# Later query loads and the adapter on the GpSimd queue, stores split into four pieces

## The chip, the cores and the metric

The kernel runs on one core of a Trainium2 chip. The metric is device time in microseconds of one launch, from inputs in device memory to outputs in device memory. The core has five engines that run side by side, each with its own instruction stream in order: TensorE (PE in the profile, with its weight loads as PEld), VectorE (DVE), ScalarE (ACT), GpSimd (POOL) and SyncE (SP), which here only issues transfers. Transfers are issued on the queues of SP, ACT and POOL and carried out by 16 DMA engines. Results of TensorE land in PSUM; everything else lies in SBUF.

## The reference

Two stages, in float32. The first is a retention layer on q, k, v of shape (8 batches, 8 heads, 576 positions, 64): scores are scaled by 1/8, multiplied by a decay gamma_h^(i-j) for i >= j and zero otherwise, and applied to v without a softmax. Its output, seen as x of 4608 tokens by 512 columns, goes into a mixture of adapters: 8 experts of rank 16.

```
scores = scale * q @ k.T                      # per batch and head
ret    = scores * Dmat                        # gamma_h ** (i - j), i >= j, else 0
x      = (ret @ v) as (4608, 512)
logits = x @ w_gate                           # 8 experts
top 2 experts per token, softmax weights w over these two
out    = x + sum over the two: w * ((x @ A[e]) @ B[e])
```

## The kernel before, in words

The positions are cut into chunks of 128, four full ones and a rest of 64. A *unit* is one chunk of two batches (for the rest chunk, of four batches), with all 8 heads; there are 18 units, numbered 0 to 17, in two runs of nine. The decay is split into factors of rows and columns, so that the unit's keys are scaled once (`k_scale`, L226, in place in the loaded tile) and the output once (`xT_out`, with the tables gx). What earlier chunks add is kept as a running state W per batch and head.

For a unit u the work is:

- loads of q, k and v into natural tiles of 256 KB per batch, two transfers per tensor and unit (`load`, `load_batch`, L139 to L169). The tiles have 3, 4 and 4 buffers; `freed(u, name)` (L171) is the point at which the tile of unit u is free, and issues the load of unit u + 3 (queries) or u + 4 (keys, values) into its buffer. All of these are on SP's queue, except two of unit 0's on ACT's.
- `k_scale` on GpSimd, then transposes of keys and queries on TensorE (`T_mm`, L248), copied out by ScalarE (`k_out`, `q_out`, `qs_out`) into kT, M and Qs. `q_turn` (L271) copies half of Qs into M; it is on GpSimd (L185, M<-Qs).
- scores (`S0_mm` L322, `S1_mm` L304), masked by VectorE into M and S1 (L373, L360).
- `W_values` and `V1_copy` put v beside the state on GpSimd (L185, W<-v and V<-v); `U_mm` (L395) makes k^T v, which `U_out` adds to the state of the chunk behind it: one half on VectorE, the other by a ScalarE copy and a GpSimd add (L188, W<-pn,W).
- outputs x^T (`O_mm` L432, `O1_mm` L451), scaled by VectorE; router and adapter product in one (`Z_mm`, L487) against AW, which holds A and w_gate; the routing on VectorE and ScalarE; B applied and x added back (`Y_mm` L605, `B_mm` L620); osb copied out and stored (`store`, L691).

The order on every engine is written out by hand: the order of the calls in the program is the order of each engine's stream, and waits follow from data. Units 0 to 3 are written out one by one (L803 to L948); from r = 2 on, a loop (L954) works on unit r's outputs, unit r + 1's scores and unit r + 2's transposes. The last two units' outputs stand behind the loop.

The adapter A is loaded once into An and put into the layout of AW by TensorE (`A_select`, L514) with a selection table sel, which `A_select_open` (L496) builds on GpSimd from ident: a memset and 16 small copies (L503). Bcat and Wg are the two loads on GpSimd's queue. W has zero halves for the first chunks, written by four memsets (L207) for units 0 and 1.

The lines ahead of the first scores of unit 0, where the changed loads are issued:

```
    load(1, "k")
    load(1, "q")
    nc.sync.dma_start(
        out=An.rearrange("p e i r -> p e (i r)"),
        in_=moe_A.rearrange("e (a i) r -> a e (i r)", i=4),
    )
    load(1, "v")
    ...
    for nm, u in (("k", 2), ("q", 2), ("v", 2), ("k", 3), ("q", 3), ("v", 3)):
        load(u, nm)
```

Of the kernel before, what the change touches and what calls it, by code (L numbers as in the profile page):

```python
# [17 lines left out]
HALF = (LO, HI)  # L18
# [3 lines left out]
def kernel(  # L22
# [10 lines left out]
    nc = tc.nc  # L33
    B, H, S, Dh = q.shape
    Ntok, Dm = out.shape
    E = moe_w_gate.shape[1]
    R = moe_A.shape[2]
    ER = E * R
# [57 lines left out]
    ident = cpool.tile([128, 128], FP32, tag="ident", name="ident")  # L96
# [12 lines left out]
    AW = rest.tile([128, HP, ER + E], FP32, tag="AW", name="AW")  # L109
    Bcat = cpool.tile([128, Dm], FP16, tag="Bcat", name="Bcat")  # L110
    ident16 = rest.tile([128, 128], FP16, tag="ident16", name="ident16")
    warm = rest.tile([128, 1], FP32, tag="warm", name="warm")
    An = cpool.tile([128, E, 4, R], FP32, tag="An", name="An")
    Wg = rest.tile([128, HP, E], FP32, tag="Wg", name="Wg")
# [8 lines left out]
    NU = len(units)  # L123
# [15 lines left out]
    def load_batch(u, nm, b, eng=None):  # L139

        c, bp = units[u]
        return (eng or nc.sync).dma_start(  # L142
            out=nat[(nm, u)][:, b * H : (b + 1) * H, :],
            in_=srcs[nm][2 * bp + b, :, 128 * c : 128 * c + 128, :].rearrange("h j d -> j h d"),
        )

    def load_open(u, nm):
        nat[(nm, u)] = iop.tile(
            [128, 2 * H, Dh], FP32, tag=nm + "32", name=nm + "32", bufs=NBUF[nm]
        )  # L150

    def load(u, nm):

        if u >= NU:
            return
        load_open(u, nm)
        c, bp = units[u]
        if full(u):
            for b in range(2):
                load_batch(u, nm, b)  # L160
            return
        for par in range(2):
            b = 4 * bp + 2 * par
            nc.sync.dma_start(
                out=nat[(nm, u)][HALF[par]],
                in_=srcs[nm][b : b + 2, :, 128 * c : 128 * c + 64, :].rearrange(
                    "b h j d -> j (b h) d"
                ),
            )  # L169

    def freed(u, nm):  # L171

        load(u + NBUF[nm], nm)
# [25 lines left out]
    def W_open(u):  # L199
        n = 1 if full(u) else 2  # L200
        st[u]["W"] = [
            wk.tile([128, 2, 2, HP, Dh], FP32, tag=f"W{x}", name=f"W{x}", bufs=(5, 2)[x])
            for x in range(n)
        ]
        if units[u][0] == 0:
            for p in range(2):
                nc.gpsimd.memset(st[u]["W"][0][HALF[p], p], 0.0)  # L207

    def W_values(eng, u, ps=(0, 1)):
        vt = nat[("v", u)]  # L210
# [5 lines left out]
    def V1_copy(eng, u):  # L216

        s = st[u]
        s["V1"] = wk.tile([64, 2, HP, Dh], FP32, tag="V1", name="V1", bufs=2)
        for b, src in enumerate(heads(nat[("v", u)][HI], 0)):  # L220
            copy(eng, s["V1"][:, b], src)

    def k_scale(eng, u, bs=slice(0, 2)):
        c = units[u][0]
        kt = nat[("k", u)].rearrange("p (b h) d -> p b h d", b=2)[:, bs]
        eng.tensor_tensor(  # L226
            out=kt, in0=kt,
            in1=gv[:, c, :].unsqueeze(1).unsqueeze(3).broadcast_to(
                (128, bs.stop - bs.start, H, Dh)
            ),  # L230
            op=ALU.mult,
        )
# [38 lines left out]
    def q_turn(eng, u, p):  # L271

        s = st[u]
        copy(
            eng, s["M"][HALF[p], p, 1],
            s["Qs"][HALF[1 - p]].rearrange("p a r i -> p a (r i)"),
        )
# [202 lines left out]
    def Z_open(u, tag="F"):  # L480
        st[u]["pz"] = bank(tag, [128, 2, ER + E], name="pz")
# [14 lines left out]
    def A_select_open(eng):  # L496


        eng.memset(sel, 0.0)
        for g in range(2):  # L500
            for e in range(2):
                for i in range(4):
                    eng.tensor_copy(  # L503
                        out=sel[HALF[g], e, i, :].rearrange("p (a x) -> p a x", x=4)[:, :, i],
                        in_=ident[HALF[g], 64 * g + 32 * e : 64 * g + 32 * e + 32],
                    )

    def A_select(tags, engs):

        pa = [bank(t, [128, 2, E, R], name="pa") for t in tags]  # L510
        for e in range(2):
            for i in range(4):
                for g in range(2):
                    mm(  # L514
                        pa[g][:, e].rearrange("p a r -> p (a r)"),
                        lhsT=sel[HALF[g], e, i, :],
                        rhs=An[HALF[g], :, i, :],
                        start=(e == 0 and i == 0),
                        stop=(i == 3),
                        skip_group_check=True,  # L520
                    )
        for g in range(2):
            copy(
                engs[g], AW[:, 2 * g : 2 * g + 2, 0:ER],
                pa[g].rearrange("p e a r -> p e (a r)"),
            )
# [164 lines left out]
    def store(u):  # L691
        c, bp = units[u]
        of = st[u]["osb"]
        tok = out.rearrange("(b s) d -> s b d", s=S)
        if full(u):
            for n in range(2):
                nc.sync.dma_start(
                    out=tok[128 * c : 128 * c + 128, 2 * bp + n, :], in_=of[:, n, :]
                )
            return  # L700
        for par in range(2):
            b = 4 * bp + 2 * par
            nc.sync.dma_start(
                out=tok[128 * c : 128 * c + 64, b : b + 2, :], in_=of[HALF[par]]
            )
# [98 lines left out]
    for b in range(2):  # L804
        d = load_batch(0, "v", b)
        if b == 0:
# [4 lines left out]
                ),  # L811
                reason="first keys and queries",
            )
    load(1, "k")
    load(1, "q")
    nc.sync.dma_start(
        out=An.rearrange("p e i r -> p e (i r)"),
        in_=moe_A.rearrange("e (a i) r -> a e (i r)", i=4),
    )
    load(1, "v")  # L820
    T_first("q", 0, "S")
    for p in range(2):
        copy(
# [6 lines left out]
    T_first("q", 1, "EF")  # L830
    for r in range(2):
        copy(nc.scalar, s0["Qs"][:, :, r], pt[("q", 1)][r])
    for nm, u in (("k", 2), ("q", 2), ("v", 2), ("k", 3), ("q", 3), ("v", 3)):
        load(u, nm)
    T_first("k", 1, "R")
    k_first(1)
# [10 lines left out]
    W_values(nc.gpsimd, 0, (0,))  # L847
    W_values(nc.scalar, 0, (1,))
    V1_copy(nc.gpsimd, 0)
    A_select_open(nc.gpsimd)  # L850
    k_scale(nc.vector, 1)
    U_mm(0)
    freed(0, "k")
# [8 lines left out]
    k_out(nc.scalar, 1)  # L862
    T_open(1, "q", "R")
    T_mm(1, "q")
    freed(1, "q")
    q_out(nc.vector, 1, 0)
    for b in range(2):
        xT_out(0, slice(b, b + 1))
# [1 line left out]
    qs_out(nc.scalar, 1)  # L870
    for p in range(2):
        q_turn(nc.gpsimd, 1, p)
    A_select("EF", (nc.scalar, nc.scalar))
    nc.gpsimd.tensor_copy(out=AW[:, :, ER : ER + E], in_=Wg)
    nc.gpsimd.tensor_copy(out=ident16, in_=ident)
    S0_mm(1, "S")
    S1_mm(1, "R")
    for b in range(2):
# [2 lines left out]
    S1_mask(1)  # L881
    W_values(nc.gpsimd, 1)
    V1_copy(nc.gpsimd, 1)
    Z_open(0)
    Z_mm(0)
    U_mm(1)
# [18 lines left out]
    k_out(nc.scalar, 2)  # L905
    T_open(2, "q", "S")
    T_mm(2, "q")
    freed(2, "q")
    q_out(nc.scalar, 2, 0)
    q_out(nc.scalar, 2, 1)  # L910
    qs_out(nc.scalar, 2)
    for p in range(2):
        q_turn(nc.gpsimd, 2, p)
    Z_open(1, "E")
    Z_mm(1)
    route_a(1)
# [19 lines left out]
    k_out(nc.scalar, 3)  # L936
    T_open(3, "q", "R")
    T_mm(3, "q")
    freed(3, "q")
    q_out(nc.scalar, 3, 0)  # L940
    q_out(nc.scalar, 3, 1)
    qs_out(nc.scalar, 3)
# [2 lines left out]
    V1_copy(nc.gpsimd, 3)  # L945
    for p in range(2):
        q_turn(nc.gpsimd, 3, p)
    k_scale(nc.gpsimd, 4)  # L948


# [3 lines left out]
    for r in range(2, END):  # L954
        nxt, nn = r + 1, r + 2
        if full(nxt):
            U_mm(nxt, "E" if r > 2 else "F")
        freed(nxt, "k")
        if full(nxt):
            U_out(nxt)  # L960
        O_mm(r)
        O1_mm(r)
        freed(r, "v")
        if full(nxt):
            xT_out(r)
        else:
            for b in range(2):
                xT_out(r, slice(b, b + 1))
        if full(nxt):
            S1_mm(nxt, "R")  # L970
            S1_mask(nxt)
        S0_mm(nxt)
        for p in range(2):
            S0_mask(nxt, p)
        X_mm(r - 1)
        zT_out(r - 1)
        Z_open(r)
        Z_mm(r)
        route_a(r)
        early = nn < NU and not full(nn)  # L980
        if not early:
            Y_mm(r - 1, "R")
        if nn < NU:
            if "W" not in st[nn]:
                W_open(nn)
            T_open(nn, "k", "A")
            T_mm(nn, "k")
            k_out(nc.scalar, nn)
        if early:
            Y_mm(r - 1, "R")  # L990
        route_s(r)
        B_mm(r - 1)
        osb_open(r - 1)
        osb_out(nc.vector if nn < NU else nc.scalar, r - 1)
        store(r - 1)
        if nn < NU:
            T_open(nn, "q", "S")
            T_mm(nn, "q")
            freed(nn, "q")
            q_out(nc.scalar, nn, 0)  # L1000
            q_out(nc.scalar, nn, 1)
            qs_out(nc.scalar, nn)
            W_values(nc.gpsimd, nn)
            if full(nn):
                V1_copy(nc.gpsimd, nn)
            for p in range(2):
                q_turn(nc.gpsimd, nn, p)
            if nn + 1 < NU:
                k_scale(nc.gpsimd, nn + 1)
            if r < 2 * NFULL and r % 2 == 0:  # L1010
                gx_of(r // 2 + 1)
        route_b(r)
# [81 lines left out]
```

## Time and profile before

| what | value |
|---|---|
| median of 3 runs | 185.77 us |
| all runs | 183.97, 185.77 and 916.15 us |
| the profiled execution's own time | 183.94 us |
| its span | 182.2 us |
| instructions | 9356 |
| moved by DMA | 39.00 MB, mean 214 GB/s |
| read and written in device memory | 29.09 MB and 9.44 MB |

The span runs from the first to the last instruction of one profiled execution; the 1.74 us around it belong to the execution's own time. Busy shares are of the span. In the lines by slices, each digit is the busy share of one fortieth of the span, 4.6 us, in tenths; PEclk is the granted clock of TensorE. A timeline row is: start, duration, engine, line, operation, output<-input with shapes, how many are merged, and in brackets how long the engine sat idle before it and what ended that. `x2` rows are two instructions merged.

### The profile page before, as it was taken

The numbers are of one execution on the slowest core, as the hardware profiler recorded it, in microseconds if no ns is written. First come the engines' busy times: TensorE is split into PE (matmuls) and PEld (weight loads), VectorE is DVE, ScalarE is ACT, GpSimd is POOL, SyncE is SP. The second block draws the span as 40 slices with busy tenths as digits, with TensorE's granted clock in tenths as the row PEclk, the third lists the DMA queues.
The fourth block names the chain that finished last, engine by engine and source line by source line (L and its number), as shares of the span: only waits on it lengthen the run. The fifth ranks groups of instructions, "written<-read, shape, count | busy, mean of one in ns | idle before, by whom it ended". The sixth has DMA issues, their size and how long they took to land.

```text
span 182.2 us, 9356 instructions
## 1 busy us (share of the span) xinstructions
PE 173.1 (95%) x4126; PEld 157.8 (87%) x4126; DVE 128.8 (71%) x232; ACT 76.3 (42%) x156; POOL 125.1 (69%) x214
## 2 busy tenths in 40 slices
PE   7998999599999999999999999999999999999980
PEld 6797998498999899998999999999999999989960
DVE  4494763718686869696868596969696969687770
ACT  0734164910707070706273634343444444443330
POOL 7396984998297959796987747858677777792000
PEclk9999999969999999999999999999999999999997
DMA  4999899899997979999989798989999999923125
GB/s 115 288 229 211 182 199 206 181 235 227 219 286 175 255 176 267 219 288 230 270 185 271 173 293 193 258 183 246 220 286 232 264 202 271 273 84 119 55 107 189
DMA packets 119368, 39.00 MB, mean 214 GB/s; under 512 B 114320, under 2 KB 114720, under 8 KB 119328
## 3 DMA queue, kind: packets, MB, share of 16 engines
q1 hardware_dynamic: 116480, 37.30, 82.9%
q10 hardware_dynamic: 2672, 0.96, 2.1%
q8 instruction: 32, 0.52, 1.1%
q0 software_dynamic: 176, 0.15, 0.5%
q14 instruction: 8, 0.07, 0.1%
HBM read 29.09 MB, written 9.44 MB: 212 GB/s over the span
## 4 chain that ended last, share of the span: by engine, by line
PE 87%; POOL 4%; DMA 3%; SPq 2%; DVE 0%; issue 0%; DVEq 0%
PE pz L487 18%; PE px L432 17%; PE pu L395 9%; PE ps L322 8%; PE pt_k L248 5%; PE px L451 5%; PE po L620 5%; PE pt_q L248 4%; PE po L605 4%; PE ps L304 4%; PE pf L723 3%; DMA v<-in_v_dram 3%; SPq L142 2%; PE pzt L587 2%; POOL sel L503 2%; PE pa L514 1%
## 5 line engine op out<-in xcount | busy, mean ns | idle before, releaser
L373 DVE TENSOR_TENSOR M<-ps,tri 64x1024 f32<-64x1024 f32 (+1 forms) x34 | 37.3, 1097 | 3.8 <-PE ps L322 3.1
L487 PE MATMUL pz<-AW,xT 128*128 128x136 f32 x288 | 37.7, 284 | 0.0
L226 POOL TENSOR_TENSOR k<-k,pack 128x1024 f32<-128x1024 f32 (+1 forms) x18 | 32.5, 1806 | 6.6 <-PE pt_k L779 2.9
L185 POOL COPY M<-Qs 64x512 f32<-64x512 f32 x36 | 21.9, 609 | 21.9 <-ACT Qs L183 16.1
L432 PE MATMUL px<-M,W 128*64 128x128 f32 (+1 forms) x640 | 36.1, 268 | 0.0
L185 POOL COPY W<-v 64x256 f32<-64x256 f32 x78 | 29.2, 395 | 10.0 <-DMA v<-in_v_dram 6.8
L487 PEld LDWEIGHTS pz<-AW,xT 128*128 128x128 f32 x288 | 34.6, 190 | 0.4
L183 ACT COPY kT<-pt_k 128x1024 f32<-128x1024 f32 x17 | 17.2, 1015 | 40.1 <-PE pt_k L248 40.1
L432 PEld LDWEIGHTS px<-M,W 128*64 128x64 f32 x640 | 32.8, 141 | 0.2
L470 DVE TENSOR_TENSOR xT<-px,gx 128x1024 f32<-128x1024 f32 x11 | 13.5, 1225 | 17.8 <-PE px L451 13.4
L185 DVE COPY osb<-po 128x1024 f32<-128x1024 f32 (+2 forms) x18 | 19.2, 1075 | 5.9 <-PE po L620 5.0
L596 ACT COPY zT<-pzt 128x256 f16<-128x256 f16 (+1 forms) x19 | 6.9, 361 | 37.7 <-PE pzt L587 37.7
L183 ACT COPY M<-pt_q 64x512 f32<-64x512 f32 x35 | 20.2, 577 | 1.8 <-DVE M L185 0.7
L395 PE MATMUL pu<-v,k 128*64 128x64 f32 x512 | 19.2, 229 | 1.6 <-DMA v<-in_v_dram 1.6
L395 PEld LDWEIGHTS pu<-v,k 128*64 128x64 f32 x512 | 16.8, 141 | 3.0 <-ACT kT L183 1.4
L322 PE MATMUL ps<-Qs,kT 64*64 64x128 f32 (+1 forms) x304 | 17.9, 259 | 0.0
L322 PE MATMUL ps<-M,kT 64*64 64x128 f32 (+1 forms) x304 | 17.9, 259 | 0.0
L188 POOL TENSOR_TENSOR W<-pn,W 64x512 f32<-64x512 f32 x12 | 15.2, 1270 | 0.9
L322 PEld LDWEIGHTS ps<-M,kT 64*64 64x64 f32 x304 | 14.8, 134 | 0.2
L322 PEld LDWEIGHTS ps<-Qs,kT 64*64 64x64 f32 x304 | 14.8, 134 | 0.0
L248 PEld LDWEIGHTS pt_k<-ident,k 64*128 64x128 f32 x272 | 9.8, 138 | 3.7 <-issue 2.5
L248 PE MATMUL pt_k<-ident,k 64*128 64x64 f32 x272 | 12.1, 229 | 0.5 <-POOL k L226 0.5
(73 smaller groups left out, 295.7 us busy)
## 6 DMA issues: line engine op xcount, KB each, us to landing
q<-in_q_dram SPq DMA_DIRECT2D x36, 256.0 KB, 5.2
v<-in_v_dram SPq DMA_DIRECT2D x36, 256.0 KB, 4.7
k<-in_k_dram SPq DMA_DIRECT2D x34, 256.0 KB, 4.7
out_dram<-osb SPq DMA_DIRECT2D x34, 256.0 KB, 4.6
k<-in_k_dram ACTq DMA_DIRECT2D x2, 256.0 KB, 4.9
An<-in_moe_A_dram SPq DMA_DIRECT2D x1, 256.0 KB, 5.4
out_dram<-osb ACTq DMA_DIRECT2D x2, 128.0 KB, 2.8
out_dram<-osb SPq DMA_DIRECT2D x2, 128.0 KB, 2.9
```

Source lines behind the costliest of these rows:

```text
L183: nc.scalar.copy(out=out, in_=in_)
L185: eng.tensor_copy(out=out, in_=in_)
L188: eng.tensor_tensor(out=out, in0=a, in1=b, op=ALU.add)
L226: eng.tensor_tensor(out=kt, in0=kt, in1=gv[:, c, :].unsqueeze(1).unsqueeze(3).broadcast_to((128, bs.stop - bs.start, H, Dh)), op=ALU.mult,)
L248: mm(ps[:, r, hp, b, :], lhsT=src[HALF[r], b * H + 2 * hp : b * H + 2 * hp + 2, :], rhs=ident[HALF[r], 64 * r : 64 * r + 64], is_transpose ...
L322: mm(s["ps0"][HALF[1 - p], b, hp, sl], lhsT=s["kT"][HALF[ho], x, hp, b, :], rhs=Q_of(u, b, ho, hp, sl), start=(hp == 0 and x == 0), stop=True,
L373: nc.vector.tensor_tensor(out=s["M"][sl, p, bs].rearrange("p b a i -> p (b a) i"), in0=s["ps0"][sl, bs].rearrange("p b a i -> p (b a) i"), ...
L395: mm(s["pu"][HALF[p], b, hp, :], lhsT=nat[("k", u)][:, h, :], rhs=nat[("v", u)][:, h, :], start=(hp == 0 and b == 0), stop=True, skip_grou ...
L432: mm(s["pxb"][b][HALF[ho], hp, sl], lhsT=s["W"][x][:, p, b, hp, :], rhs=s["M"][:, p, b, hp, sl], start=(hp == 0 and x == 0), stop=True, sk ...
L451: mm(s["px"][HALF[ho], b, hp, HI], lhsT=vv, rhs=s["S1"][HALF[p], b, hp, :], start=False, stop=True, skip_group_check=True,)
L470: nc.vector.tensor_tensor(out=s["xT"][:, bs].rearrange("p b a i -> p b (a i)"), in0=s["px"][:, bs].rearrange("p b a i -> p b (a i)"), in1= ...
L487: mm(s["pz"][:, n, :], lhsT=s["xT"][:, n, dt, :], rhs=AW[:, dt, :], start=(dt == 0), stop=(dt == HP - 1), skip_group_check=True,)
```

## The change

- Queries of units 2 and later are loaded by GpSimd's queue, not SP's. Each load stands at another place of the order: unit 2's behind unit 1's `q_turn`, unit 3's behind unit 1's `V1_copy`, unit 4's behind unit 2's `q_turn`, those of 5 and 6 behind unit 3's `q_turn` and ahead of `k_scale` of unit 4; in the loop the load stands behind `q_turn` (that is, behind `V1_copy` on GpSimd) and ahead of the next `k_scale`.
- The adapter A is loaded by GpSimd's queue, behind `V1_copy` of unit 0.
- `A_select_open`, the copy of Wg into AW and ident16 stand at the head of GpSimd's stream; the memsets of W of units 0 and 1 are on VectorE.
- In the loop, `q_turn` is on ScalarE.
- A full unit's two stores (128 rows each) become four, of 104 and 24, and of 88 and 40 rows, except for the last two units.

```
@@ load
+        eng = nc.gpsimd if nm == "q" and u > 1 else nc.sync
...
-                load_batch(u, nm, b)
+                load_batch(u, nm, b, eng)
...
-            nc.sync.dma_start(
+            eng.dma_start(
@@ W_open
-                nc.gpsimd.memset(st[u]["W"][0][HALF[p], p], 0.0)
+                (nc.vector if u < 2 else nc.gpsimd).memset(st[u]["W"][0][HALF[p], p], 0.0)
@@ store
-            for n in range(2):
-                nc.sync.dma_start(
-                    out=tok[128 * c : 128 * c + 128, 2 * bp + n, :], in_=of[:, n, :]
-                )
+            for n, cut in enumerate((104, 88)):
+                for a, b in ((0, cut), (cut, 128)) if u < NU - 2 else ((0, 128),):
+                    nc.sync.dma_start(
+                        out=tok[128 * c + a : 128 * c + b, 2 * bp + n, :], in_=of[a:b, n, :]
+                    )
@@ start
-    load(1, "k")
-    load(1, "q")
-    nc.sync.dma_start(
-        out=An.rearrange("p e i r -> p e (i r)"),
-        in_=moe_A.rearrange("e (a i) r -> a e (i r)", i=4),
-    )
-    load(1, "v")
+    for nm in "kqv":
+        load(1, nm)
+    A_select_open(nc.gpsimd)
+    nc.gpsimd.tensor_copy(out=AW[:, :, ER : ER + E], in_=Wg)
+    nc.gpsimd.tensor_copy(out=ident16, in_=ident)
...
-    for nm, u in (("k", 2), ("q", 2), ("v", 2), ("k", 3), ("q", 3), ("v", 3)):
+    for nm, u in (("k", 2), ("v", 2), ("k", 3), ("v", 3)):
...
     V1_copy(nc.gpsimd, 0)
-    A_select_open(nc.gpsimd)
+    nc.gpsimd.dma_start(
+        out=An.rearrange("p e i r -> p e (i r)"),
+        in_=moe_A.rearrange("e (a i) r -> a e (i r)", i=4),
+    )
...
     T_mm(1, "q")
-    freed(1, "q")
...
         q_turn(nc.gpsimd, 1, p)
+    load(2, "q")
     A_select("EF", (nc.scalar, nc.scalar))
-    nc.gpsimd.tensor_copy(out=AW[:, :, ER : ER + E], in_=Wg)
-    nc.gpsimd.tensor_copy(out=ident16, in_=ident)
...
     V1_copy(nc.gpsimd, 1)
+    load(3, "q")
...
     T_mm(2, "q")
-    freed(2, "q")
...
         q_turn(nc.gpsimd, 2, p)
+    freed(1, "q")
...
     T_mm(3, "q")
-    freed(3, "q")
...
         q_turn(nc.gpsimd, 3, p)
+    freed(2, "q")
+    freed(3, "q")
     k_scale(nc.gpsimd, 4)
@@ loop
             T_mm(nn, "q")
-            freed(nn, "q")
...
             for p in range(2):
-                q_turn(nc.gpsimd, nn, p)
+                q_turn(nc.scalar, nn, p)
+            freed(nn, "q")
             if nn + 1 < NU:
                 k_scale(nc.gpsimd, nn + 1)
```

## The prediction

> **What bounds the kernel now.** I read the page first: engine shares, then the slices, then the chain that ended last.
>
> ```profile
> PE 173.1 (95%) x4126; PEld 157.8 (87%) x4126; DVE 128.8 (71%) x232; ACT 76.3 (42%) x156; POOL 125.1 (69%) x214
> PE   7998999599999999999999999999999999999980
> PEclk9999999969999999999999999999999999999997
> DMA  4999899899997979999989798989999999923125
> PE 87%; POOL 4%; DMA 3%; SPq 2%; DVE 0%; issue 0%; DVEq 0%
> ```
>
> TensorE is the bound, apart from slice 7 (half busy), slice 8 (lower clock) and the last two. The table of stretches puts times on this.
>
> ```profile
> 30.00:33.00 3.00, 2.54 (x76) 1.93 (x66) 1.29 (x3) 1.53 (x5) 1.90 (x1) 1.00 0.82 188
> 33.00:36.24 3.24, 1.55 (x37) 1.31 (x37) 3.06 (x7) 2.85 (x5) 2.87 (x4) 1.00 0.76 168
> 36.24:41.30 5.06, 5.06 (x108) 4.89 (x112) 0.68 (x1) 0.88 (x2) 4.85 (x8) 0.66 1.03 233
> 47.00:56.04 9.04, 9.04 (x232) 8.38 (x234) 7.09 (x13) 3.90 (x10) 6.60 (x9) 1.00 0.93 230
> 99.90:145.10 45.20, 45.20 (x1152) 41.89 (x1152) 34.82 (x60) 19.99 (x42) 32.06 (x50) 1.00 0.96 237
> ```
>
> Columns: span, busy time of PE, PE's weight loads, DVE, ACT, POOL, granted clock, DMA share, GB/s. From 47 us on TensorE is full: one unit takes 9.04 us, and five of them 45.20. Nothing in the diff touches those matmuls, so the change can gain only ahead of 47 us. There TensorE idles 0.46 + 1.69 us and then runs 5.06 us at clock 0.66, which loses (1 - 0.66) x 5.06 = 1.7 us. The TensorE timeline says what it waited for:
>
> ```profile
> 16.14 2.06 PE L514 MATMUL pa<-An,sel 64*128 64x128 f32 x32 [0.34 <-POOL sel L503]
> ...
> 25.13 0.72 PE L248 MATMUL pt_k<-ident,k 64*128 64x64 f32 x16
> ...
> 33.05 0.71 PE L248 MATMUL pt_k<-ident,k 64*128 64x64 f32 x16 [0.50 <-POOL k L226]
> ...
> 35.55 0.34 PE L395 MATMUL pu<-v,k 128*64 128x64 f32 x4 [1.29 <-DMA v<-in_v_dram]
> 36.24 1.01 PE L395 MATMUL pu<-v,k 128*64 128x64 f32 x18 [0.35 <-DMA v<-in_v_dram]
> ...
> 45.27 0.71 PE L248 MATMUL pt_k<-ident,k 64*128 64x64 f32 x16
> ```
>
> The three L248 rows are the key transposes of units 2, 3 and 4. Each needs its unit's keys scaled by Pool (L226). Without waits, unit 2 to unit 3 takes 33.05 - 0.50 - 25.13 = 7.42 us. Unit 3 to unit 4 takes 12.22, less 1.64 of waits and 1.7 of clock, so 8.88. I use the start of unit 4's key transpose, 45.27 us now, as the finish line: all behind it is 9.04 us a unit.
>
> **The change, part by part.** *Off SP's queue.* The sync queue now issues adapter and queries ahead of unit 3's values:
>
> ```profile
> 10.60 2.64 SPq L816 DMA_DIRECT2D An<-in_moe_A_dram  x1
> ...
> 25.81 3.72 SPq L142 DMA_DIRECT2D q<-in_q_dram  x2
> 29.57 1.79 SPq L142 DMA_DIRECT2D v<-in_v_dram  x2
> ```
>
> Without 2.64 and 3.72 us the values are issued over 6 us sooner, so the 1.64 us wait goes. The bytes stay, so some of this returns as sharing with the Pool queue; 1.64 of cover in 6 is enough. The rule against this part: the Trainium skill, "DMA: Bandwidth & Descriptors", section "Issuing engines are not separate DMA queues", says a second issuer gives no bandwidth, only issue time. By it the values come sooner only by order, and the sum stays; the trace, with a DMA share of 0.93 from 47 us, agrees as far as it goes.
>
> *The price on Pool.* A DMA issued by Pool is work on Pool. The trace has two:
>
> ```profile
> 1.27 0.95 POOL L732 DMA_DIRECT2D Wg<-in_moe_w_gate_dram  x1 [0.82 <-POOLq L1078]
> ...
> 23.87 0.59 POOL L890 DMA_DIRECT2D Bcat<-in_moe_B_dram  x1
> ...
> Bcat<-in_moe_B_dram POOLq DMA_DIRECT2D x1, 128.0 KB, 4.3
> ...
> Wg<-in_moe_w_gate_dram POOLq DMA_DIRECT2D x1, 16.0 KB, 4.7
> ```
>
> Bcat has 128 pieces, one row each; Wg has 512 pieces of 32 B. A query load has 1024 pieces of 256 B. If only the instruction counts, c, the cost of one, is 0.59 to 0.95. If pieces count, the two rows give 0.36 us per 384, and c = 0.95 + 512 x 0.36 / 384 = 1.43; twice Wg gives 1.9. Bounds 0.59 and 1.9. I take the middle of the two rows, 0.77: in size the load is nearer to Bcat, in pieces to Wg. This is the choice on which the time hangs.
>
> The skill's "SBUF — State Buffer", section "SBUF: two separate sides", has another price: such an issue took about 620 ns alone and 3100 behind a VectorE copy within SBUF; the page would make c 3.1 there. No run here shows it. VectorE's copies after the start read PSUM.
>
> Now Pool's order from the first q_turn of unit 1, by starts of the rows:
>
> ```profile
> 17.80 1.26 POOL L185 COPY M<-Qs 64x512 f32<-64x512 f32 x2 [1.40 <-ACT Qs L183]
> ...
> 19.63 1.51 POOL L185 COPY W<-v 64x256 f32<-64x256 f32 x4
> 21.20 0.74 POOL L185 COPY V<-v 64x256 f32<-64x256 f32 x2
> 22.03 1.90 POOL L226 TENSOR_TENSOR k<-k,pack 128x1024 f32<-128x1024 f32 x1
> ...
> 24.48 1.05 POOL L746 TENSOR_TENSOR gx<-gkx,pack 128x512 f32<-128x512 f32 x1
> ...
> 33.05 1.26 POOL L185 COPY M<-Qs 64x512 f32<-64x512 f32 x2
> 34.39 1.26 POOL L188 TENSOR_TENSOR W<-pn,W 64x512 f32<-64x512 f32 x1
> ...
> 39.49 1.90 POOL L226 TENSOR_TENSOR k<-k,pack 128x1024 f32<-128x1024 f32 x1
> ```
>
> After the change, start at 17.9 (the queries of unit 1 are no sooner). Then q_turn(1) 1.3; q(2) 2c; W(1) 1.6, V1(1) 0.8; q(3) 2c; k_scale(2) 1.9: done at 23.5 + 4c. Bcat 0.6, gx 1.1, W(2) 1.6, V1(2) 0.8, k_scale(3) 2.0: 29.6 + 4c. q_turn(2) 1.3, q(4) 2c, the add (L188) 1.3, W(3) 1.6, V1(3) 0.7, q_turn(3) 1.3, q(5) and q(6) 4c, k_scale(4) 1.9: **37.7 + 10c**. Ten query issues stand ahead of unit 4's keys, where the row at 39.49 ends at 41.4 today, 3.9 us before use.
>
> With c = 0.77 the scaled keys of unit 2 are there at 26.6 (25.13 today), of unit 3 at 32.7, of unit 4 at 45.4. TensorE: transposes of unit 2 at 26.6, of unit 3 at 34.0, ready for unit 4 at 42.9, and waits until 45.4, against 45.27: +0.1. This idle stretch, 2.5 us, is longer than the 1.69 after which the clock fell today, so I add its 1.7 us again. Behind it: per unit Pool has 6.60 - 1.25 + 1.54 = 6.9 us of 9.04 and doesn't hold TensorE again. The query issue waits there for the transposes of the queries; behind it stand the key scaling and the next add, which used to wait for the longer chain through ACT's Qs copy.
>
> *q_turn on ACT from unit 4 on.* Two copies a unit:
>
> ```profile
> 111.05 0.58 ACT L183 COPY pn<-pu 64x512 f32<-64x512 f32 x1
> 114.04 0.37 ACT L596 COPY zT<-pzt 128x256 f16<-128x256 f16 x1 [2.42 <-PE pzt L587]
> ```
>
> The pn copy comes 1.2 us later, inside the 2.42 us of idle: nothing. Without that cover 1.2 us a unit, 17 in all.
>
> *Start.* The memsets of W, 2.2 us on Pool, go to VectorE; the selection table, AW and ident16 come forward, so the 0.34 us at 16.14 goes. But the adapter now leaves Pool only behind V1(0), at about 12.2 to 13.0, and with 4.3 to 4.7 us to land it is there at 16.5 to 17.7: TensorE loses 0.4 to 1.6 us at 16.14. At c = 0.77 the key scaling of unit 2, 1.5 us late, covers it; at less than 0.6 it is what remains. VectorE and Pool also get in each other's way:
>
> ```profile
> 22.91 1.03 DVE L547 SCALAR_TENSOR_TENSOR ns<-m 128x2 f32<-128x2 f32 x1
> ...
> 28.72 0.16 DVE L547 SCALAR_TENSOR_TENSOR ns<-m 128x2 f32<-128x2 f32 x1
> ```
>
> The slow one ends with Pool's scaling at 23.93. VectorE's start tables would now meet Pool's selection copies in this way, 0 to 1.5 us; it delays the adapter more than TensorE, and is in its bound.
>
> *Stores in four.* Two more issues a unit on SP, which lost two query issues; bytes the same. I cost it at nothing; the rival below prices it.
>
> The sum: profiled execution 183.94 us (span 182.2 and 1.74 around it) + 0.1 + 1.7 = **185.7**. This sits on the profiled execution; the median shown, 185.77 (183.97 to 916.15), is 1% above it, and about 2% is what a measurement of this kernel can tell from no change.
>
> **The rivals.** *Cheap issues* (c up to 0.6). Unit 4's keys are scaled by 43.7, at most. TensorE could be there at 25.13 + 0.4 to 1.6 + 7.42 + 8.88 = 41.8 to 43.0, without idle stretch or clock loss. That is 1.6 to 3.5 us sooner, 180.5 to 182.3. For it: Bcat's 0.59 for the same order of bytes. Against: Wg's 0.95 for fewer.
>
> *Pieces count* (c about 1.43; it decides from c = 0.95). The keys of unit 4 come at 37.7 + 14.3 = 52.0: +6.7, with the clock 190.6 to 192.3, slower. In the loop Pool would then need 8.2 us of 9.04, still inside. At c = 0.95 it is 47.2 and 1.7 of clock, 187.5. For it: the only two rows rise with the pieces. Against: the Wg row is the first of its kind on Pool.
>
> *Stores on fewer DMA engines.* Rows of 104, 24, 88 and 40 may not spread evenly.
>
> ```profile
> 16.20:21.70 5.50, 5.50 (x114) 5.18 (x114) 3.85 (x7) 1.81 (x4) 3.83 (x12) 1.00 0.87 197
> ...
> 176.00:180.00 4.00, 1.11 (x13) 0.55 (x12) 1.61 (x4) 0.86 (x3) 0.00 (x0) 0.99 0.69 240
> ```
>
> Loads alone run at 197 / 0.87 = 226 GB/s full, stores alone at 348. A unit's 1.57 MB in and 0.52 MB out are 6.9 + 1.5 = 8.4 us of 9.04. If the stores lie on 13, 12, 11 and 10 engines, the fullest ten carry 8 + 2 + 8 + 4 = 22 rows for 16: 6.9 + 2.1 = 9.0, just at the limit. Were Pool's query loads a tenth slower in the engines as well, 0.2 us a unit over 14 units adds 3: 188.7. The Trainium skill, "DMA: Bandwidth & Descriptors", "Why a DMA increments its semaphore by 16 and not by 1", says the engines are the largest number up to 16 that divides the rows, which is these four counts; no trace here shows it.
>
> **How the numbers follow.** Forecast (c from 0.6 to 0.95, 183.9 to 187.5): 0.45. Cheap issues: 0.22. Pieces count: 0.25. Stores at the limit: 0.08. Range 180.8 to 191.5. Faster by over 2% (under 180.3) is the best end of the cheap case: 0.13. Slower by over 2% (over 187.6): pieces, stores and the forecast's edge: 0.37. Within: 0.50.
>
> **What would show it.** Right: Pool's query rows at 0.6 to 0.95 us; no wait for v at unit 3; TensorE waiting for k L226 at units 2 and 4; one stretch of lower clock behind; 9.04 us a unit after 47. Wrong: Pool rows of 1.4 us, a wait for An over 1.6 us, stretches over 9.1 us in the middle with waits for DMA, or slack at unit 4's keys.

## The result: slower, and where the time went

The changed kernel takes 191.48 us (189.86 to 193.93, 4 runs) beside 186.48 us of the kernel before on the same chip, a ratio of 1.043 (95% interval 1.032 to 1.054). Run again on another chip, it took 189.79 beside 185.41: 1.026 (1.016 to 1.036). The profiled execution has a span of 188.1 us; before it was 182.2, so 5.9 us are to be found. Medians here take in all runs; the ratios leave out disturbed executions, so the two can differ.

The page of the changed kernel: shares, slices, chain.

```profile
PE 175.0 (93%) x4126; PEld 159.4 (85%) x4126; DVE 134.2 (71%) x236; ACT 94.1 (50%) x184; POOL 134.9 (72%) x215
...
PE   7998969995999999999998999899999999999990
...
PEclk9999996999699999999999999999999999999997
...
PE 75%; POOL 9%; DVE 4%; ACT 4%; issue 3%; DMA 2%; SPq 0%; DVEq 0%; POOLq 0%
```

Before, one slice was at the lower clock; now there are two, with a slice ahead of each in which TensorE is less than full. Pool's share of the chain has gone from 4% to 9%, and "issue", time without a cause in the profile, is at 3%. TensorE's timeline names the waits.

```profile
16.13 2.06 PE L515 MATMUL pa<-An,sel 64*128 64x128 f32 x32 [0.33 <-DMA An<-in_moe_A_dram]
...
26.83 0.71 PE L249 MATMUL pt_k<-ident,k 64*128 64x64 f32 x16 [1.64 <-POOL k L227]
...
47.25 0.71 PE L249 MATMUL pt_k<-ident,k 64*128 64x64 f32 x16 [2.53 <-POOL k L227]
...
99.54 0.27 PE L305 MATMUL ps<-M,kT 64*64 64x64 f32 x1 [0.98 <-issue]
```

The wait for unit 3's values isn't there. In its place TensorE waits for scaled keys, at unit 2 and, longer, at unit 4. Line numbers are one higher than before. Why the keys are late is in Pool's timeline, start and duration first:

```profile
19.02 1.76 POOL L142 DMA_DIRECT2D q<-in_q_dram  x2
20.77 1.53 POOL L186 COPY W<-v 64x256 f32<-64x256 f32 x4
22.36 0.75 POOL L186 COPY V<-v 64x256 f32<-64x256 f32 x2
23.05 1.76 POOL L142 DMA_DIRECT2D q<-in_q_dram  x2
24.88 1.90 POOL L227 TENSOR_TENSOR k<-k,pack 128x1024 f32<-128x1024 f32 x1
...
34.03 1.84 POOL L142 DMA_DIRECT2D q<-in_q_dram  x2
...
41.70 3.53 POOL L142 DMA_DIRECT2D q<-in_q_dram  x4
45.30 1.90 POOL L227 TENSOR_TENSOR k<-k,pack 128x1024 f32<-128x1024 f32 x1
```

Each scaling of keys (L227) ends just ahead of the transposes above: 26.78 and 47.20. Right ahead of both stand query issues. What an issue costs is in Pool's groups:

```profile
L142 POOL DMA_DIRECT2D q<-in_q_dram x28 | 25.2, 902 | 12.8 <-PE pt_q L249 12.6 <-issue 0.2
...
L851 POOL DMA_DIRECT2D An<-in_moe_A_dram x1 | 0.9, 947 | 0.0
L735 POOL DMA_DIRECT2D Wg<-in_moe_w_gate_dram x1 | 0.9, 932 | 0.8 <-POOLq L1082 0.8
L893 POOL DMA_DIRECT2D Bcat<-in_moe_B_dram x1 | 0.6, 602 | 0.0
```

The table of stretches (span, busy time of PE, weight loads, DVE, ACT, POOL, granted clock, DMA share, GB/s) sorts the rest. The rows at clock 0.50 and 0.51 follow the two waits for keys.

```profile
28.40:31.80 3.40, 3.40 (x19) 3.15 (x19) 0.12 (x2) 1.84 (x4) 3.17 (x8) 0.50 0.89 181
44.70:47.25 2.55, 0.03 (x1) 0.00 (x0) 2.48 (x4) 0.00 (x0) 2.43 (x2) 1.00 0.91 257
48.80:52.20 3.40, 3.40 (x54) 3.33 (x52) 2.31 (x5) 3.31 (x8) 3.32 (x8) 0.51 1.16 304
57.85:93.04 35.19, 35.19 (x890) 32.36 (x890) 27.51 (x48) 20.14 (x39) 30.26 (x44) 1.00 0.94 233
93.04:103.25 10.21, 9.23 (x232) 8.43 (x232) 7.18 (x13) 5.76 (x11) 9.26 (x18) 1.00 0.99 253
112.30:122.09 9.79, 9.31 (x232) 8.45 (x232) 7.80 (x16) 5.15 (x10) 7.20 (x10) 1.00 0.93 235
```

The same two units in the kernel before, in the same table:

```profile
89.49:98.16 8.67, 8.67 (x231) 8.11 (x230) 6.49 (x12) 4.38 (x9) 7.91 (x15) 1.00 0.89 224
116.25:125.30 9.05, 9.05 (x231) 8.38 (x231) 7.09 (x13) 3.91 (x8) 6.65 (x10) 1.00 0.93 217
```

So of the 5.9 us, 2.0 are there when unit 4's keys are transposed (47.25 against 45.27). 1.6 come in the unit behind it, at the lower clock, which takes 10.6 us up to 57.85 for 9.04. And 1.5 + 0.7 come in the two units of 10.21 and 9.79 us, most of it in gaps that no wait explains. The remaining 0.1 is in smaller pieces.

### The profile page after: what moved, and what is told of

Read it like the earlier page. It is cut to its first block, busy times and chain, and to the rows that moved or that the text cites. A ratio compares the mean times of both kernels' runs of the same rounds, so it can differ in the third digit from the quotient of the medians.

```text
span 188.1 us, 9337 instructions
## 1 busy us (share of the span) xinstructions
PE 175.0 (93%) x4126; PEld 159.4 (85%) x4126; DVE 134.2 (71%) x236; ACT 94.1 (50%) x184; POOL 134.9 (72%) x215
## 3 DMA queue, kind: packets, MB, share of 16 engines
q1 hardware_dynamic: 82370, 28.65, 62.5%
q0 software_dynamic: 2816, 8.80, 16.5%
## 4 chain that ended last, share of the span: by engine, by line
PE 75%; POOL 9%; DVE 4%; ACT 4%; issue 3%; DMA 2%; SPq 0%; DVEq 0%; POOLq 0%
PE pz L488 16%; PE px L433 15%; PE pu L396 8%; PE ps L323 6%; PE pt_k L249 5%; PE po L621 5%; PE px L452 4%; PE pt_q L249 4%; PE po L606 4%; PE ps L305 3%; POOL q L142 3%; DMA q<-in_q_dram 2%; POOL k L227 2%; PE pzt L588 2%; POOL W L186 1%
## 5 line engine op out<-in xcount | busy, mean ns | idle before, releaser
L488 PE MATMUL pz<-AW,xT 128*128 128x136 f32 x288 | 39.5, 292 | 0.5 <-issue 0.5
L488 PEld LDWEIGHTS pz<-AW,xT 128*128 128x128 f32 x288 | 36.1, 196 | 1.1 <-issue 0.7
L142 POOL DMA_DIRECT2D q<-in_q_dram x28 | 25.2, 902 | 12.8 <-PE pt_q L249 12.6
L227 POOL TENSOR_TENSOR k<-k,pack 128x1024 f32<-128x1024 f32 (+1 forms) x18 | 32.5, 1804 | 1.3 <-PE pt_k L782 0.2
L396 PEld LDWEIGHTS pu<-v,k 128*64 128x64 f32 x512 | 17.1, 144 | 1.3 <-issue 0.3
L184 ACT COPY M<-Qs 64x512 f32<-64x512 f32 x28 | 17.3, 617 | 0.6
L249 PEld LDWEIGHTS pt_k<-ident,k 64*128 64x128 f32 x272 | 9.9, 138 | 8.0 <-POOL k L227 4.6
L249 PE MATMUL pt_k<-ident,k 64*128 64x64 f32 x272 | 12.1, 229 | 4.7 <-POOL k L227 4.2
```

The lines of the kernel that those rows point to most:

```text
L142: return (eng or nc.sync).dma_start(out=nat[(nm, u)][:, b * H : (b + 1) * H, :], in_=srcs[nm][2 * bp + b, :, 128 * c : 128 * c + 128, :].r ...
L184: nc.scalar.copy(out=out, in_=in_)
L227: eng.tensor_tensor(out=kt, in0=kt, in1=gv[:, c, :].unsqueeze(1).unsqueeze(3).broadcast_to((128, bs.stop - bs.start, H, Dh)), op=ALU.mult,)
L249: mm(ps[:, r, hp, b, :], lhsT=src[HALF[r], b * H + 2 * hp : b * H + 2 * hp + 2, :], rhs=ident[HALF[r], 64 * r : 64 * r + 64], is_transpose ...
L396: mm(s["pu"][HALF[p], b, hp, :], lhsT=nat[("k", u)][:, h, :], rhs=nat[("v", u)][:, h, :], start=(hp == 0 and b == 0), stop=True, skip_grou ...
L488: mm(s["pz"][:, n, :], lhsT=s["xT"][:, n, dt, :], rhs=AW[:, dt, :], start=(dt == 0), stop=(dt == HP - 1), skip_group_check=True,)
```

## The experiments

Three theories stood at the start. **A**: Pool's query issues delay the keys, and the clock falls behind each wait. **B**: the four stores load some DMA engines more. **C**: Pool's large transfers delay the fetching of instructions in the middle. A ratio is always to the kernel before on the same chip.

**Keys first.** The changed kernel with three of the early loads moved:

```
-    load(3, "q")                     # behind V1_copy of unit 1
     k_scale(nc.gpsimd, 2)
+    load(3, "q")
...
-    freed(2, "q")
-    freed(3, "q")
     k_scale(nc.gpsimd, 4)
+    freed(2, "q")
+    freed(3, "q")
```

> The changed kernel with unit 3's queries issued behind the key scaling of unit 2, and those of units 5 and 6 behind the key scaling of unit 4; nothing else differs. Theory A (Pool's query issues of 0.9 us stand ahead of the keys, TensorE idles 1.6 and 2.5 us there, and each stretch is followed by a window of halved clock): unit 2's keys are ready 1.8 us sooner, unit 4's key transposes start near 43 us, not 47.25, no window of lower clock behind them, 3 to 5 us less than the changed kernel, about 187 us. Theory B (the four stores load some DMA engines more, and the delay is there): no change, 191. Theory C (Pool's large packets delay instruction fetches in the middle): the early part improves, gaps of 0.5 to 1 us in the middle remain.

Measured: 187.65 us beside 187.49, a ratio of 1.011 (0.995 to 1.028). TensorE's waits in its trace (total, times, longest):

```profile
PE po L606 <- DMA Bcat<-in_moe_B_dram: 2.0, 1, 2.0
...
PE pt_k L249 <- POOL k L227: 1.2, 1, 1.2
PE pt_q L249 <- issue: 1.1, 1, 1.1
PE ps L305 <- issue: 1.0, 2, 0.7
```

No wait for keys is left at units 2 and 4; the one of 1.2 us is at unit 5, behind the query issues that now come after unit 4's keys. Unit 4's transposes start at 43.86, and no window of lower clock follows. A new wait of 2.0 us appeared: Bcat, behind unit 3's queries in Pool's order, lands late. Theory A holds for the early part, and by the ratios most of the loss against before is gone (1.011, where the changed kernel had 1.043 and 1.026 on other chips). The gaps in the middle stay, as C expected.

**Whole stores.** The changed kernel with one store of 128 rows a batch:

```
-            for n, cut in enumerate((104, 88)):
-                for a, b in ((0, cut), (cut, 128)) if u < NU - 2 else ((0, 128),):
+            for n in range(2):
...
```

> The changed kernel with its two whole stores a unit, of 128 rows each. Theory A: within 1 us of the changed kernel. Theory B: 2 to 4 us faster. Theory C: within 1 us, gaps without a named cause still in the middle.

Measured: 191.79 us, ratio 1.032 (1.018 to 1.046). The changed kernel itself was at 1.043 and 1.026. Theory B, which had 2 to 4 us less here, falls. Its trace bears on theory A too; TensorE's waits, and the granted clock by slices:

```profile
PE pt_k L249 <- POOL k L227: 4.9, 2, 3.1
PE ps L305 <- issue: 2.7, 3, 1.3
PE pt_q L249 <- issue: 2.0, 2, 1.4
...
PEclk9999999999999999999999999999999999999999
```

TensorE waited 3.1 us for unit 4's keys, longer than the 2.53 of the changed kernel, and the clock never fell. So the part of theory A by which the clock falls behind each wait does not hold. The kernel lost its time in the waits and in 4.7 us of gaps without a cause.

**All but the queries.** The query loads go back to the sync queue and their places of before; everything else of the change stays.

```
-        eng = nc.gpsimd if nm == "q" and u > 1 else nc.sync
+        eng = nc.sync
...
-    for nm, u in (("k", 2), ("v", 2), ("k", 3), ("v", 3)):
+    for nm, u in (("k", 2), ("q", 2), ("v", 2), ("k", 3), ("q", 3), ("v", 3)):
...
             T_mm(nn, "q")
+            freed(nn, "q")
```

> All of the change but the queries: these are issued by the sync queue at their places of before. The adapter on Pool's queue, the selection table early, the copies of Qs on ACT and the four stores stay. Theory A: no waiting for the keys, so no slower than before: 182 to 186. Theory B: 187 or more, since the four stores are there. Theory C: as A, and no gaps in the middle, since Pool moves nothing there.

Measured: 188.36 us (184.51 to 190.99) beside 187.49, no interval. In its trace (the same view of waits):

```profile
PE pu L396 <- DMA v<-in_v_dram: 3.7, 5, 1.5
PE pa L515 <- DMA An<-in_moe_A_dram: 1.7, 1, 1.7
...
PE ps L305 <- issue: 1.4, 2, 1.0
```

No wait for keys, as A says, but the time is above the 182 to 186 us that A gave, and without an interval it can't be told from before. And there are waits for values in the middle, and 1.4 us without a cause although Pool moves nothing there. So C, that Pool's transfers are what makes those gaps, falls in this form, as far as one trace shows it.

**The four stores alone,** put into the kernel before:

```
-            for n in range(2):
+            for n, cut in enumerate((104, 88)):
+                for a, b in ((0, cut), (cut, 128)) if u < NU - 2 else ((0, 128),):
...
```

> The kernel before with the four stores alone. Theory A: within 1 us of before. Theory B: 2 us or more slower than before, with TensorE waiting for loads after 47 us.

Measured: 186.39 us beside 187.49 in 10 runs, ratio 0.984 (0.970 to 0.997). It isn't slower; that it is faster, which no theory expected, rests on its two lowest runs. The trace also shows something about the kernel before. No store has been issued by 42 us, so up to there this is the kernel before, and yet unit 3's values are not late:

```profile
33.01 0.71 PE L248 MATMUL pt_k<-ident,k 64*128 64x64 f32 x16
33.53 0.70 PE L248 MATMUL pt_q<-ident,q 64*128 64x64 f32 x16
34.16 1.15 PE L395 MATMUL pu<-v,k 128*64 128x64 f32 x32
...
41.68 0.53 PE L248 MATMUL pt_k<-ident,k 64*128 64x64 f32 x10
```

And in its waits:

```profile
PE ps L304 <- issue: 3.3, 3, 1.8
PE pu L395 <- DMA v<-in_v_dram: 2.3, 6, 0.5
```

It takes 8.67 us from unit 3 to unit 4, where the profiled execution of before took 12.22. The wait for values and the lower clock behind it, which the prediction took for something to gain, are thus not in every execution.

**The changed kernel again,** beside the next three:

> The changed kernel itself, beside the three others on one chip. Theory A: unit 4's key transposes near 47 us behind a wait of about 2.5 us for the scaled keys, two windows of halved clock, 4 to 5 us above the kernel before.

Measured: a ratio of 1.026, as given above. The keys again: unit 4's transposes at 46.19 behind a wait of 3.14 us. One window of lower clock, not the two that were expected.

**Waits filled.** Dummy matmuls in the two waits for keys:

```
+    fill(5, "R", 128)
     T_open(2, "k", "R")
...
+            if nn == 4:
+                fill(8, "A", 128)
             T_open(nn, "k", "A")
```

> The changed kernel with dummy matmuls in the two waits for the keys: 5 of them (1.45 us at the rate of those at the start) ahead of unit 2's key transposes, 8 (2.3 us) ahead of unit 4's. They do work that the result doesn't need and finish inside the waits. If the lower clock behind the waits comes from TensorE's idling, the two windows of halved clock go and the time falls by 2 to 3.4 us, while the keys stay as late as before (27 and 47 us). If the clock has another cause, the windows stay and the time doesn't change.

The table of stretches, first of this kernel and then of the changed kernel run beside it, for the unit behind the late keys:

```profile
26.93:34.47 7.54, 7.42 (x167) 6.47 (x168) 2.66 (x9) 4.14 (x8) 7.18 (x12) 1.00 1.00 223
46.33:55.37 9.04, 9.04 (x230) 8.38 (x230) 6.23 (x9) 5.14 (x10) 8.73 (x12) 1.00 1.01 283
```

```profile
46.19:57.25 11.06, 10.79 (x231) 10.00 (x231) 6.82 (x10) 5.17 (x10) 10.65 (x16) 0.85 1.00 276
```

The keys are as late (46.33), the lower clock is gone, and the unit takes 9.04 us for 11.06. So where the lower clock came behind a wait, it cost 1.6 us (10.60 for 9.04) to 2.0. That idling brings it fits these two traces, but isn't shown by them alone: the kernel with whole stores idled 3.1 us in this place and kept its clock. The Trainium skill, "TensorE: Matmul & The Clock Gate", Part 1, gives about 3.4 us of idling as what brings half rate, and about 3.4 us of work as what ends it. The length agrees with the changed kernel, whose granted clock is 0.50 from 28.4 to 31.8 and from 48.8 to 52.2 and 1.00 on both sides; in the kernel without stores, below, it was twice that, 6.8 us. The idle time does not agree: the waits ahead were of 1.64 and 2.53 us.

The whole kernel wasn't faster, as it should have been by 2 to 3.4 us: 191.12 us, ratio 1.031 (1.022 to 1.041) beside 1.026. About 1 us of that lies outside the span (2.4 to 2.8 us in its four runs, 1.7 to 1.8 in those of the changed kernel). Its trace also has 2.0 us of gaps without a cause ahead of the query transposes (L249); whether these ate the gain can't be told from 4 runs.

**Idle places.** All of the change, with unit 2's queries behind the adapter, where Pool idled 4.7 us, Bcat ahead of unit 3's queries, and units 3, 5 and 6 behind the keys as above:

```
     # An on Pool's queue, behind V1_copy of unit 0
+    load(2, "q")
...
     k_scale(nc.gpsimd, 2)
     nc.gpsimd.dma_start(out=Bcat, in_=moe_B.rearrange("e r d -> (e r) d"))
+    load(3, "q")
```

> All of the change, with Pool's early query issues at places where Pool idles or nothing urgent stands behind: unit 2's right behind the adapter, where Pool idled 4.7 us, unit 3's behind the key scaling of unit 2 and the load of Bcat, those of units 5 and 6 behind the key scaling of unit 4. Theory A: no wait for scaled keys at units 2 and 4, no wait for Bcat, unit 4's key transposes at 42 to 44 us, 5 us under the changed kernel and 0 to 2 us under the kernel before. If the early transfer of unit 2's queries delays unit 1's values or unit 2's keys, a wait of 1 to 2 us for a DMA shows at unit 1's or 2's matmuls.

Measured: 186.27 us beside 185.41, ratio 1.004 (0.999 to 1.009), 12 runs: well under the changed kernel's 1.026 on the same chip, but not under the kernel before, as was expected. The waits in its trace:

```profile
PE pt_k L249 <- POOL k L227: 1.7, 2, 1.1
PE pt_q L249 <- issue: 1.3, 1, 1.3
```

The transposes of unit 4 are at 42.61, within the range that was expected, behind a wait of 0.61 us that was not. The longer of the two waits for keys is at unit 5: Pool now issues the queries of 5, 6 and, in the loop, 7, six issues, between the scaling of unit 4's keys and of unit 5's.

**The loop's queries on the sync queue,** in addition: Pool issues those of units 2 to 6 only.

```
-        eng = nc.gpsimd if nm == "q" and u > 1 else nc.sync
+        eng = nc.gpsimd if nm == "q" and 1 < u < 7 else nc.sync
...
             T_mm(nn, "q")
+            freed(nn, "q")
...
-            freed(nn, "q")
```

> As the kernel with idle places, but queries of unit 7 and later are issued by the sync queue at their places of before; Pool issues those of units 2 to 6 only. Theory A alone: as with idle places, within 1 us. If Pool's queue helps the middle by bringing values in time, waits for values come back there and it is 1 to 3 us slower than with idle places; if Pool's transfers delay the middle, it is faster by as much.

Measured: 183.03 us beside 185.41, ratio 0.988 (0.982 to 0.995): 1.2% faster than before, and about 1.5% under the kernel with idle places on the same chip; the two intervals don't overlap. The waits:

```profile
PE ps L305 <- issue: 0.9, 1, 0.9
PE pt_k L249 <- POOL k L227: 0.7, 1, 0.7
PE pt_q L249 <- DMA q<-in_q_dram: 0.5, 1, 0.5
```

So Pool's query issues cost something in the loop. Two issues less ahead of unit 5's keys are part of it, since the wait of 1.1 us there is gone; what the rest is, was not separated. Whether Pool's queue is worth something for the first units isn't shown either: this kernel has the rest of the change too.

**No stores** (the changed kernel):

```
     def store(u):
+        if u < NU - 2:
+            return
```

> The changed kernel without the stores of all units but the last two; it leaves that part of the output unwritten, so its time is that of a kernel with 8.4 MB fewer to move. Theory A: the late keys stay, unit 4's key transposes at 46 to 47.5 us behind a wait for the scaling, and the halved clock behind it, since no store had been issued by then. If the gaps without a named cause in the middle come from the full DMA engines, they go, and 1 to 2 us with them; if not, they stay.

Measured: 187.94 us (187.15 to 190.24, 10 runs), ratio 1.010 (1.006 to 1.013). Waits, and then the table of stretches over the middle:

```profile
PE pt_k L249 <- POOL k L227: 3.7, 2, 3.1
```

```profile
47.00:145.00 98.00, 98.00 (x2465) 90.72 (x2461) 73.32 (x124) 57.40 (x111) 80.45 (x118) 0.98 0.76 179
```

The keys are late as ever (45.72, a wait of 3.15), so the stores are not what delays them; the granted clock at that wait is 0.50 from 45.0 to 51.8. From 47 us on the DMA engines are at a share of 0.76 instead of 0.94, and TensorE has no gap in 98 us. So the gaps of the middle went with the stores. By the ratios the time fell by 3 us and more, where 1 to 2 were expected. Full engines alone don't make such gaps, though: the profile of before has none, at a share of 0.96. That it is the fetching of instructions which waits there is argued only: nothing in the traces shows what TensorE lacked.

**Unit 6 later, with four stores and with two.** From the kernel with the loop on the sync queue, unit 6's queries behind unit 5's keys (unit 7's, on the sync queue, move with them); then the same with whole stores.

```
     freed(2, "q")
-    freed(3, "q")
...
             T_mm(nn, "q")
+            if nn > 4:
+                freed(nn, "q")
...
                 k_scale(nc.gpsimd, nn + 1)
+            if nn == 4:
+                freed(3, "q")
+                freed(4, "q")
```

> As the kernel with the loop's queries on the sync queue, with the queries of unit 6 issued by Pool behind the key scaling of unit 5, not of unit 4. Theory A: 1.8 us of Pool's work less ahead of unit 5's keys, so any wait there goes; 0 to 1 us less than the kernel with the loop's queries on the sync queue, which was 0.988 of before.

> The same with two whole stores a unit. If the four pieces cost nothing and bring nothing (theory A), the ratio to before is the same within 0.01. If the pieces load some DMA engines more (theory B), it is 1% or more faster than the one with four; if they bring something, slower by as much.

Measured: 183.55 us, ratio 0.986 (0.981 to 0.992), and 186.04 us, 0.984 (0.977 to 0.990), both beside 186.28. The later place brings nothing more that can be measured. The ratios agree within 0.01, as expected for four pieces that cost and bring nothing; by their intervals a difference of up to about 1% either way isn't excluded. The gain of the four stores alone, 0.984 with an interval up to 0.997, was not seen again.

## Why the prediction was wrong

The forecast was 185.7 us, 1% above the profiled execution and inside what counts as no change; the kernel is 4.3% slower, just inside the upper end of the range. That end belongs to the rival "pieces count", whose price no run showed, so lying inside it is luck. The profiled execution took 189.86 us, 4.2 over the forecast. Step by step:

- **What bounds it: right in kind.** The finish line (unit 4's key transposes), Pool's order ahead of it and the three gating keys are what the trace shows. With the measured price, 0.90, the sums give 27.1, 33.2 and 46.7 for the scaled keys of units 2, 3 and 4; the trace has 26.8, 32.8 and 47.2.
- **The price c: mis-sized.** 0.77 was taken as the middle of two rows, between 0.59 and 0.95; it measures 0.90, and no issue of Pool's in the trace took over 0.97. Ten of them stand in the sum, so 0.13 became 1.3 us, and 0.5 more remained of a wait of 1.03 us, of the add for ACT's copy, which the sum left out. Together that is 1.8 of the 4.2 us. The rival "pieces count" was wrong in its reason: 1024 pieces (0.95 for An, 0.90 for queries) cost no more than 512 (0.93 for Wg). Bcat, 128 rows, is the odd one.
- **The clock: right in size, in part by luck,** 1.6 for 1.7. There were two such windows, but the first fell where TensorE was to wait for Pool anyway. The second profile of the same kernel had one window, and with whole stores none came, behind waits of 1.75 and 3.1 us; the step from "longer than 1.69 us" to a lower clock does not hold each time.
- **"Behind it all is 9.04 us a unit": the step that failed.** The prediction took the profiled execution's middle, without a gap, as given. The changed kernel's profile lost 2.2 of the 4.2 us there, in two units of 10.21 and 9.79 us, most of it in gaps that no wait explains. What the steps give without this term, 45.27 to 47.25 and 1.6, is 187.5, 1.9% over. The gaps are not the change's alone: the kernel with only the four stores has 3.3 us of them ahead of its scores (L304), and the traces of all the other kernels with stores, ten of them, have 0.9 to 4.7 us. Only the profile of before and that of the kernel without stores have none. What makes the gaps stays open.
- **What was to be gained: not there to gain each time.** The 1.64 us wait for values and its 1.7 us of clock were in the one profile shown, and not in the other one that ran the same instructions up to there. The runs of before lie between 183.6 and 190.3, one of 916.15 apart, with medians from 185.41 to 187.49 by chip; the sum started from one of 183.94. Against ordinary runs of before, it is the late keys that weigh most: moving the early issues alone took the ratio from 1.026 to 1.004 on one chip, with 2.1 us of gaps still in the trace.
- **Stores, adapter, ACT: right,** as far as it can be told. Four stores cost nothing that these runs can measure. TensorE began on the adapter at 16.1 in one profile and at 17.1 in the second, with waits of 0.33 and 1.29 us. No wait for the copies of Qs showed on TensorE.

## What to carry to other kernels

A transfer issued by an engine that also computes is work on that engine: give it a row in the sum, and look at what stands behind it in that engine's order. It cost 0.9 us here, ten times ahead of unit 4's keys; with the first units' loads at places where less stood behind them, the loss was nearly gone. And take a sum from one profile only for what repeats: a second trace that runs the same instructions showed that one of the waits and its lower clock did not, and every later trace with stores had gaps that the first one lacked.

## What the runs showed of the hardware

The changed kernel's DMA queues, packets, MB and share of 16 engines:

```profile
DMA packets 87897, 38.99 MB, mean 207 GB/s; under 512 B 80738, under 2 KB 81138, under 8 KB 87858
...
q1 hardware_dynamic: 82370, 28.65, 62.5%
q0 software_dynamic: 2816, 8.80, 16.5%
```

Pool's queue moved 8.80 MB in 2816 packets; before, when it moved 0.15 MB, the whole kernel had 119368 packets for 39.00 MB. It took 16.5 / 8.80 = 1.88% of the engines' time a MB, the sync queue 62.5 / 28.65 = 2.18%: 14% less. The sync queue's part holds stores too; with nearly all of them left out it was 48.5 / 20.26 = 2.39% a MB, beside 16.4 / 8.80 = 1.86%. I had priced both alike. A gain from it didn't show in the time.
